# More block products and a written-out order in a fused attention and GLU kernel

## The chip, the cores and the metric

The kernel runs on one core of one Trainium2 chip. The metric is the device time of one execution in microseconds (us); a kernel's figure is the median of its runs. A core has TensorE (PE in the profile; it loads weights and multiplies), VectorE (DVE), ScalarE (ACT), GpSimd (POOL) and SyncE (SP), which here issues all DMAs. Each takes its own instructions strictly in order and waits for the others by semaphores.

## The reference, cut to what matters

```python
# x: 1 x 2048 x 512, H = 32 heads of 16, F = 1792, all bf16
xn = layernorm(x)
q, k, v = split(xn @ wqkv)                       # 512 -> 3 * 512
phi(t) = concat(softmax(t @ w_phi), softmax(-(t @ w_phi)))   # per head, 16 -> 32 features
kv = phi(k)^T v ; z = sum over tokens of phi(k)
attention = (phi(q) kv) / (phi(q) z + 1e-6)
glu = ((xn @ w_gate) * (xn @ w_up)) @ w_down     # 512 -> 1792 -> 512
out = x + attention @ wo + glu
```

`kv` sums over all 2048 tokens, so no attention output exists before the last token's k features do. The two GLU products are independent of the attention.

## The kernel before

The 2048 tokens are 16 tiles of 128 (`NT`), in four groups of 512 (`GT` = 4 tiles). The 512 channels are 4 chunks of 128 (`DC`), the 1792 hidden columns 14 chunks (`FC`), in two halves of 7 (`FH`). A matmul here has 128 x 128 weights and up to 512 columns; its f32 result goes to a PSUM bank, and six banks in turn (`bank`) serve most products.

The program is emitted in Python order, and each engine keeps the order in which its instructions were emitted (`manual_schedule`). In stages:

- **Start** (to about 12 us): layernorm of tiles 0 to 3, transposes, first v tiles, while weights arrive.
- **k stage** (lines 604 to 679): for each token tile `vkproj` projects v and k; `features` (lines 288 to 306) makes two exponentials on ScalarE (294, 296), a sum of 16 and a reciprocal on VectorE (300, 302) and the product on GpSimd (304); `kv(n)` adds to the two `kv` banks. Between them `ffn(1)` makes one unit of gate and up for groups 0 and 1 (28 units, `half`, line 350): four matmuls each of 512 columns for gate and for up, a copy on ScalarE (356) and a multiplication on VectorE (362). `weight_norm` (420, ScalarE) sums weights for power-of-two scales.
- **Attention and output**: `attend(n)` makes one tile's attention and sends it through a transposing DMA; `fin_parts(n)` (387) adds 14 matmuls of `w_down` and 4 of `wo`, all 512 columns wide, and stores a tile.
- **Block stage** (`run_blocks`): gate and up of groups 2 and 3 (tokens 1024 to 2047) use a two-by-two block product with seven products in place of eight (`pair_block`, line 487: two tokens' halves by two channel halves by two hidden halves). Its operands are differences: of weights, `T` (`weight_sums`, line 445, 28 steps of 512 columns on VectorE and GpSimd, after ScalarE has scaled the weights, 435), and of tokens, `ss` (454). The results are joined by copies on ScalarE (493, 495), additions on VectorE (499, 503) and, for the second factor, a multiplication from two SBUF operands on GpSimd or VectorE (504).
- **End**: output tiles 9 to 15, one `q_begin`/`attend`/`fin` round each; the last tile's output is stored in two pieces, of 384 and 128 columns.

Of the kernel before, what the change touches and what calls it, by code (L numbers as in the profile page):

```python
# [15 lines left out]
PSUM = bass.MemoryType.PSUM  # L16


def _bcast_ap(ap_in: bass.AP, new_ap):
    return bass.AP(tensor=ap_in.tensor, offset=ap_in.offset, ap=new_ap)  # L20


@with_exitstack
def kernel(
# [40 lines left out]
    consts = ctx.enter_context(tc.tile_pool(name="consts", bufs=1))  # L65
    wpool = ctx.enter_context(tc.tile_pool(name="wpool", bufs=1))
# [7 lines left out]
    wgu = wpool.tile([P, 2, DC, F], BF16)  # L74
# [60 lines left out]
    xnT = xpool.tile([P, DC, HALF], BF16)  # L135
# [11 lines left out]
    for i in range(NV):  # L147
        vt = vpool.tile([P, 8, 4, E1], BF16, name=f"vt{i}", tag="vt")
        nc.vector.memset(vt[:, :, :, DH:E1], 1.0)
        vts.append(vt)  # L150
# [9 lines left out]
    def bank(name, dt=F32, n=TT):  # L160
        return ps_s.tile([P, n], dt, name=name, tag="s")
# [3 lines left out]
    def xt(n):  # L165
        return xnT[:, :, n * P:(n + 1) * P] if n < QT else x16[:, :, (n - QT) * P:(n - QT + 1) * P]
# [21 lines left out]
    def subtract(n, *means):  # L188
        xns[n] = xnpool.tile([P, D], BF16, name="xn", tag="x")
        nc.vector.tensor_scalar(out=xns[n][:], in0=xall[:, n, :], scalar1=means[0],  # L190
                                scalar2=means[1] if len(means) > 1 else None, op0=ALU.subtract,
                                **(dict(op1=ALU.subtract) if len(means) > 1 else {}))
# [9 lines left out]
    def centre_by_halves(n):  # L202
        h = D // 2
        part = consts.tile([P, 2], F32)
        junk = xnpool.tile([P, 2, h], BF16, name="junk", tag="x")
# [5 lines left out]

    chores = []

    def chore(k=1):
        for _ in range(min(k, len(chores))):
            chores.pop(0)()

    def ln_block(lo):
        mv = mv_tile()
        nb = lnpool.tile([P, GT], F32, name="nb", bufs=GT)  # L220
        rstd = []

        def scales():
            r = lnpool.tile([P, GT], F32, name="rstd", bufs=GT)
            ln_rstd(mv, GT, r[:])
            nm = lnpool.tile([P, GT], F32, name="nm")
            nc.gpsimd.tensor_scalar(out=nm[:], in0=mv[:, :, 0], scalar1=-1.0, scalar2=None, op0=ALU.mult)
            nc.gpsimd.tensor_tensor(out=nb[:], in0=nm[:], in1=r[:], op=ALU.mult)
            rstd.append(r)

        def apply(i):
            late = lo + i >= QT
            xn = xnpool.tile([P, D], F16 if late else BF16, name="xn", tag="x")
            if late:
                nc.gpsimd.tensor_scalar(out=xn[:], in0=xall[:, lo + i, :], scalar1=rstd[0][:, i:i + 1],
                                        scalar2=nb[:, i:i + 1], op0=ALU.mult, op1=ALU.add)
            else:
                nc.scalar.activation(out=xn[:], in_=xall[:, lo + i, :], func=AF.Identity,
                                     scale=rstd[0][:, i:i + 1], bias=nb[:, i:i + 1])
            nc.sync.dma_start(out=xt(lo + i), in_=xn[:], transpose=True)  # L240

        for i in range(GT):
            chores.append(lambda i=i: ln_stats(lo + i, mv[:, i, :]))
        chores.append(scales)
        for i in range(GT):
            chores.append(lambda i=i: apply(i))
# [18 lines left out]
    def fold(qk, dst, j0):  # L265
        R = P // 2
        banks = [bank("pq").rearrange("p (j c x) -> p j c x", j=2, c=DC) for r in range(2)]
        for j in range(2):
            for c in range(DC):
                for r in range(2):  # L270
                    rows = slice(r * R, (r + 1) * R)
                    nc.tensor.matmul(banks[r][:, j, c, :], lhsT=wT2[rows, qk, c, (j0 + j) * P:(j0 + j + 1) * P],  # L272
                                     rhs=bd[rows, c, 4 * r:4 * r + 4, :].rearrange("p a b -> p (a b)"),
                                     start=True, stop=True)
        dv = dst[:, j0:j0 + 2, :].rearrange("p j (c r x) -> p r j c x", c=DC, r=2)
        nc.scalar.copy(out=dv[:, 0], in_=banks[0])
        nc.vector.tensor_copy(out=dv[:, 1], in_=banks[1])

    def fold_both(qk, dst):
        for j0 in (0, 2):  # L280
            fold(qk, dst, j0)
# [6 lines left out]
    def features(n, w, name, pf=None):  # L288
        if pf is None:
            pf = bank(name)  # L290
            proj(pf, n, w)
        e = epool.tile([P, NG, 2, 4 * DH], F32, name="e")
        pfv = pf.rearrange("p (g c) -> p g c", g=NG)
        nc.scalar.activation(out=e[:, :, 0, :], in_=pfv, func=AF.Exp,  # L294
                             scale=rst[:, n:n + 1] if n < GT else 1.0)
        nc.scalar.activation(out=e[:, :, 1, :], in_=pfv, func=AF.Exp,  # L296
                             scale=nrst[:, n:n + 1] if n < GT else -1.0)
        ev = e[:].rearrange("p g s (h f) -> p (g s h) f", f=DH)
        sums = epool.tile([P, 2 * H], F32, name="sums")
        nc.vector.tensor_reduce(out=sums[:], in_=ev, axis=AX.X, op=ALU.add)  # L300
        rs = epool.tile([P, 2 * H, 1], F32, name="rs")
        nc.vector.reciprocal(out=rs[:].rearrange("p a b -> p (a b)"), in_=sums[:])  # L302
        phi = epool.tile([P, NG, P], BF16, name=f"phi{name}", tag="phi", bufs=4)
        nc.gpsimd.tensor_tensor(out=phi[:].rearrange("p g (x f) -> p (g x) f", f=DH), in0=ev,  # L304
                                in1=rs[:].to_broadcast((P, 2 * H, DH)), op=ALU.mult)
        return phi

    sends = []

    def qproj(n, held=False, new_bank=bank):  # L310
        q_begin(n, new_bank)
        q_end(held)

    q_open = []

    def q_begin(n, new_bank):
        pf = new_bank("q")
        proj(pf, n, W1q, lower)
        q_open.append((n, pf))

    def q_end(held=False):
        q_rest()
        q_features(held)

    def q_rest():
        n, pf = q_open[0]
        proj(pf, n, W1q, upper)

    def q_features(held=False):
        n, pf = q_open.pop()  # L330
        phiq = features(n, W1q, "q", pf)

        def send():
            phiqTs[n] = qtpool.tile([P, NG, P], BF16, name="phiqT")
            nc.sync.dma_start(out=phiqTs[n][:], in_=phiq[:].rearrange("p g c -> p (g c)"), transpose=True)

        sends.append(send)
        if not held:
            qsend()

    def qsend():
        sends.pop(0)()

    hTs = {}
    units = [(T, f) for T in range(NGRP // 2) for f in range(FC)]

    def half(w, name, T, f, lo, hi):
        ps = bank(name)[:, 0:hi - lo]
        for c in range(DC):
            nc.tensor.matmul(ps, lhsT=w[:, c, f * P:(f + 1) * P], rhs=xnT[:, c, T * TT + lo:T * TT + hi],  # L350
                             start=(c == 0), stop=(c == DC - 1))
        return ps

    def gate_copy(ps, n):
        g_sb = gpool.tile([P, TT], BF16, name="g_sb")
        nc.scalar.copy(out=g_sb[:, 0:n], in_=ps)  # L356
        return g_sb

    def hidden(T, f, ps, g_sb, lo, hi):
        if T not in hTs:  # L360
            hTs[T] = hpool.tile([P, FC, TT], BF16, name="hT", tag="h")
        nc.vector.tensor_tensor(out=hTs[T][:, f, lo:hi], in0=ps, in1=g_sb[:, 0:hi - lo], op=ALU.mult)  # L362

    def unit(T, f, lo=0, hi=TT):
        pg = half(wg, "g", T, f, lo, hi)
        pu = half(wu, "u", T, f, lo, hi)
        hidden(T, f, pu, gate_copy(pg, hi - lo), lo, hi)

    def ffn(k):
        for _ in range(k):  # L370
            if units:
                unit(*units.pop(0))

    def fin_parts(n, new_bank, lo=0, hi=D):
        T, t4 = n // GT, n % GT
        w = hi - lo
        held = []

        rows = [(hTs[T][:, f, t4 * P:(t4 + 1) * P], wd[:, f, lo:lo + w]) for f in range(FC)]
        rows += [(oTs[n][:, c, :], wo[:, c, lo:lo + w]) for c in range(DC)]  # L380
        if n == 2 * GT:
            rows = [row for f, row in enumerate(rows) if f % FH != FH - 1 or f >= FC] + [rows[FH - 1], rows[FC - 1]]

        def mm(i):
            if i == 0:
                held.append(new_bank("fin")[:, 0:w])
            nc.tensor.matmul(held[0], lhsT=rows[i][0], rhs=rows[i][1], start=(i == 0), stop=(i == len(rows) - 1))  # L387
            if i == len(rows) - 1:
                store(held[0])
# [444 lines left out]
```

## Time and profile before

| | us |
|---|---|
| median of 3 runs | 216.08 |
| lowest and highest | 215.33, 216.12 |
| the profiled execution | 215.67 |
| its span, first to last instruction | 213.9 |
| PE busy in it | 210.1 (98%) |
| DVE, ACT, POOL busy | 163.2, 125.0, 129.2 |
| granted clock of TensorE | 1.00 |

The profile is one execution, by hardware trace. Its page gives busy time by engine and a chain of work that ended last; answers of the trace give groups of instructions (count, busy time, mean ns of one, idle time before them and what ended it), windows (busy time of each engine between two moments) and timelines (start, duration, engine, line, tiles). Consecutive instructions of an engine overlap a little, so their spacing, start to start, is shorter than the duration shown.

### The profile page before, as it was taken

The numbers are of one execution on the slowest core, as the hardware profiler recorded it, in microseconds if no ns is written. First come the engines' busy times: TensorE is split into PE (matmuls) and PEld (weight loads), VectorE is DVE, ScalarE is ACT, GpSimd is POOL, SyncE is SP. The second block draws the span as 40 slices with busy tenths as digits, with TensorE's granted clock in tenths as the row PEclk, the third lists the DMA queues.
The fourth block names the chain that finished last, engine by engine and source line by source line (L and its number), as shares of the span: only waits on it lengthen the run. The fifth ranks groups of instructions, "written<-read, shape, count | busy, mean of one in ns | idle before, by whom it ended". The sixth has DMA issues, their size and how long they took to land.

```text
span 213.9 us, 3610 instructions
## 1 busy us (share of the span) xinstructions
PE 210.1 (98%) x1280; PEld 101.7 (48%) x1280; DVE 163.2 (76%) x279; ACT 125.0 (58%) x219; POOL 129.2 (60%) x112
## 2 busy tenths in 40 slices
PE   8999999999999999999999999999999999999994
PEld 3664445444444444554444444444444444444543
DVE  5757979869867788887777897988969689776341
ACT  4635578998896999442666686868746352220000
POOL 3600557597895788859899497979788620333000
PEclk9999999999999999999999999999999999999999
DMA  5999995613022023234444202021120201333511
GB/s 152 266 281 385 374 287 87 91 26 75 0 51 52 0 49 81 66 40 112 100 101 100 49 0 52 0 74 25 48 49 3 74 26 34 91 98 98 126 49 49
DMA packets 47249, 19.91 MB, mean 93 GB/s; under 512 B 37504, under 2 KB 46976, under 8 KB 47104
## 3 DMA queue, kind: packets, MB, share of 16 engines
q1 hardware_dynamic: 47232, 19.69, 36.6%
q8 instruction: 10, 0.16, 0.3%
q14 instruction: 7, 0.06, 0.1%
HBM read 8.67 MB, written 2.10 MB: 50 GB/s over the span
## 4 chain that ended last, share of the span: by engine, by line
PE 98%; ACT 1%; DVE 0%; issue 0%
PE fin L387 29%; PE g L350 11%; PE u L350 11%; PE sa L487 11%; PE pv L285 7%; PE q L285 6%; PE k L285 6%; PE sc L487 6%; PE sb L487 3%; PE kv L622 2%; PE ab L686 2%; PE warm L554 2%; PE pq L272 1%; PE tp L253 1%; ACT k L493 0%; ACT xnT L256 0%
## 5 line engine op out<-in xcount | busy, mean ns | idle before, releaser
L387 PE MATMUL fin<-wd,hT 128*128 128x512 bf16 (+2 forms) x238 | 54.1, 366 | 0.0
L304 POOL TENSOR_TENSOR phiq<-e,rs 128x1024 bf16<-128x1024 f32 x16 | 30.9, 1934 | 25.6 <-DVE rs L302 18.1
L304 POOL TENSOR_TENSOR phik<-e,rs 128x1024 bf16<-128x1024 f32 x16 | 30.9, 1933 | 24.2 <-DVE rs L302 17.3
L300 DVE TENSOR_REDUCE sums<-e 128x64 f32<-128x1024 f32 x32 | 38.7, 1208 | 9.0 <-ACT e L296 9.0
L350 PEld LDWEIGHTS <-wgu 128*128 128x128 bf16 x240 | 23.1, 98 | 24.2
L387 PEld LDWEIGHTS <-hT 128*128 128x128 bf16 x238 | 22.3, 98 | 24.4
L350 PE MATMUL u<-xnT,wgu 128*128 128x512 bf16 (+1 forms) x120 | 29.1, 365 | 0.0
L350 PE MATMUL g<-xnT,wgu 128*128 128x512 bf16 (+1 forms) x120 | 28.9, 365 | 0.0
L504 POOL TENSOR_TENSOR hT<-u_sb,hT 128x512 bf16<-128x512 bf16 x18 | 21.1, 1185 | 10.1 <-DVE u_sb L503 10.1
L362 DVE TENSOR_TENSOR hT<-u,g_sb 128x512 bf16<-128x512 f32 (+1 forms) x30 | 18.6, 622 | 4.5 <-PE u L350 3.9
L356 ACT CAST g_sb<-g 128x512 bf16<-128x512 f32 (+1 forms) x30 | 17.1, 569 | 8.1 <-PE g L350 7.9
L294 ACT ACTIVATE e<-q 128x512 f32<-128x512 f32 x12 | 7.2, 598 | 23.6 <-PE q L285 23.6
L302 DVE RECIPROCAL rs<-sums 128x64 f32<-128x64 f32 x32 | 17.7, 552 | 2.5
L493 ACT ACTIVATE k<-sa,both 128x512 f32<-128x512 f32 x21 | 14.5, 688 | 8.7 <-PE sa L487 8.6
L495 ACT COPY k<-sa 128x512 f32<-128x512 f32 x21 | 12.3, 587 | 11.2 <-DVE u_sb L503 7.4
L398 DVE TENSOR_TENSOR o_sb<-fin,xall 128x512 bf16<-128x512 f32 (+2 forms) x13 | 8.4, 646 | 12.0 <-PE fin L387 12.0
L445 POOL TENSOR_TENSOR T<-wgu,T 128x512 f16<-128x512 bf16 x14 | 17.0, 1216 | 0.5
L387 PE MATMUL fin<-wo,oT 128*128 128x512 bf16 (+2 forms) x68 | 17.1, 366 | 0.0
L487 PEld LDWEIGHTS <-T 128*128 128x128 f16 x112 | 10.8, 98 | 13.1 <-issue 0.6
L487 PE MATMUL sa<-ss,T 128*128 128x512 f16 x56 | 16.7, 379 | 0.1
L435 ACT ACTIVATE wgu<-wgu,up 128x1024 bf16<-128x1024 bf16 x14 | 15.9, 1156 | 0.1
L420 ACT ACTIVATE junk<-wgu 128x1024 bf16<-128x1024 bf16 x14 | 15.1, 1083 | 0.0
(98 smaller groups left out, 352.1 us busy)
## 6 DMA issues: line engine op xcount, KB each, us to landing
out_dram<-o_sb SPq DMA_DIRECT2D x15, 128.0 KB, 1.9
wd<-in_B_w_down_dram SPq DMA_DIRECT2D x1, 1792.0 KB, 15.4
wgu<-in_B_w_gate_dram SPq DMA_DIRECT2D x2, 640.0 KB, 6.8
wgu<-in_B_w_up_dram SPq DMA_DIRECT2D x2, 640.0 KB, 8.0
xall<-in_A_x_dram SPq DMA_DIRECT2D x1, 1024.0 KB, 12.1
xall<-in_A_x_dram SPq DMA_DIRECT2D x4, 128.0 KB, 2.7
vk<-in_A_wqkv_dram SPq DMA_DIRECT2D x2, 256.0 KB, 3.6
wgu<-in_B_w_gate_dram SPq DMA_DIRECT2D x2, 256.0 KB, 4.9
```

Of the source, the lines that this page charges most:

```text
L285: nc.tensor.matmul(ps, lhsT=xt(n)[:, j, :], rhs=w[:, j, :], start=(j == 0), stop=(j == DC - 1))
L300: nc.vector.tensor_reduce(out=sums[:], in_=ev, axis=AX.X, op=ALU.add)
L302: nc.vector.reciprocal(out=rs[:].rearrange("p a b -> p (a b)"), in_=sums[:])
L304: nc.gpsimd.tensor_tensor(out=phi[:].rearrange("p g (x f) -> p (g x) f", f=DH), in0=ev, in1=rs[:].to_broadcast((P, 2 * H, DH)), op=ALU.mult)
L350: nc.tensor.matmul(ps, lhsT=w[:, c, f * P:(f + 1) * P], rhs=xnT[:, c, T * TT + lo:T * TT + hi], start=(c == 0), stop=(c == DC - 1))
L356: nc.scalar.copy(out=g_sb[:, 0:n], in_=ps)
L362: nc.vector.tensor_tensor(out=hTs[T][:, f, lo:hi], in0=ps, in1=g_sb[:, 0:hi - lo], op=ALU.mult)
L387: nc.tensor.matmul(held[0], lhsT=rows[i][0], rhs=rows[i][1], start=(i == 0), stop=(i == len(rows) - 1))
L435: nc.scalar.activation(out=cols, in_=cols, func=AF.Identity, scale=up2[:, k, g:g + 1])
L445: (nc.gpsimd if i % 2 or k < 2 else nc.vector).tensor_tensor(out=t[:, i], in0=a, in1=b, op=ALU.subtract)
L487: nc.tensor.matmul(held[name], lhsT=w[:, j, :], rhs=x[:, j, :], start=start and j == 0, stop=(j == hc - 1), skip_group_check=True)
L504: (nc.vector if k == FH - 1 else nc.gpsimd).tensor_tensor(out=dst, in0=u[:], in1=dst, op=ALU.mult)
```

## The change

The program is cut into 1,244 named steps, and a string `ORDER` gives the order in which they are emitted, with the engine of many of them (`/a` ScalarE, `/v` VectorE, `/g` GpSimd); `SLOTS` gives each step's buffer. The start, up to tile 3's v projection, is as before.

Three parts of the arithmetic change. Gate and up of group 1 (tokens 512 to 1023) no longer go through units; they use the seven block products too, on halves of 256 tokens (steps with `N`). Output tiles 9, 10, 11 are paired with 13, 14, 15 (`pair_steps`), and their `w_down` part becomes seven products over half the hidden chunks and half the output columns (256), from differences of `w_down` (`c`, `w` steps, f16) and of the hidden values (`S` steps, written over the gate and up weights). Their joins are `K`, `A`, `B` and `J` steps. The scales come from sums of squares and hold for a whole weight matrix, for `w_down` too. Third, the loop that emits the steps makes the first GpSimd instruction after a VectorE step with two SBUF operands wait for that step.

```diff
+ORDER = """
+wq g3 gc3/a =k g1 fk0 gc1/a fka0/v fk2 fkv0/a fkv2/a u3 u0 fka2/v k0 u1 k1 h1 h3 kx0 ky0 kr0 ki0 kp0/g g0 g4 ky1
...
+X15 P3a.10 J3.10 X10
+"""
...
+    def hidden_sum(i, k, eng):
+        tok = slice(t0 * P, TT)
+        S = [wgu16[:, j // 2, t0:GT, ((j % 2) * FH + k) * P:((j % 2) * FH + k + 1) * P] for j in range(4)]
+        A11, A12, A21, A22 = (hT(T)[:, k + h * FH, tok].rearrange("p (t x) -> p t x", x=P) for T in (2, 3) for h in (0, 1))
+        a, b, op = ((A21, A22, ALU.add), (S[0], A11, ALU.subtract), (A11, A21, ALU.subtract), (A12, S[1], ALU.subtract))[i]
+        eng.tensor_tensor(out=S[i], in0=a, in1=b, op=op)
...
+        product(1, "a", a(2, 0), d("b11"), True)
+        keep("k1", 1, "a")
+        add("k1", "A1", lambda: x(n, 0))
+        product(2, "b", a(2, FH), B21, True, (n, 0))
+        join(2, n, 0, "b", lambda: kept("k1"))
+        product(5, "d", s(0), d("t1"), True)
...
+        product(6, "a", s(1), d("t2"))
...
+        product(3, "c", s(3), d("b22"), True, (n, 1))
...
+        product(7, "a", s(2), d("t3"))
...
+        product(4, "a", a(3, FH), d("t4"), False, (m, 0))
...
+    both_in_sbuf = re.compile(r"(N?z|t|wt|c[bt]|S|N?m|[AB]|a|ws)\d")
+    turn = None
+    for word in ORDER.split():
+        name, _, eng = word.partition("/")
+        fn, default = steps.pop(name)
+        before = len(nc.cur_bb.bb.instructions)
...
+        issued = nc.cur_bb.bb.instructions[before:]
+        on_pool = [i for i in issued if i.engine == ET.Pool]
+        on_dve = [i for i in issued if i.engine == ET.DVE]
+        if on_pool and turn is not None:
+            tc.add_manual_dep(on_pool[0], turn.name, AFTER, reason="turns")
+            turn = None
+        if on_dve and both_in_sbuf.match(name):
+            turn = on_dve[-1]
...
-    blocks = [(k, g) for k in range(FH) for g in range(2)]
...
-        for n in range(9, NT):
-            if n < 12:
-                q_begin(n + 4, bank)
-                q_rest()
-            if n + 1 < NT:
-                attend(n + 1, ps_ab)
...
-            fin(n, cuts=(0, D) if n < NT - 1 else (0, 3 * P, D))
```

The steps that the prediction names: `vk` v and k projection of a tile, `vc` its copy, `kx ky kr ki kp kv` its features and `kv` sum (`q...` the same for q), `n` a weight norm, `a` a layernorm application, `gc` a gate copy, `p`/`k`/`j`/`m`/`d` products, copies, joins, multiplications of a block (`N` the narrow ones), `t` a weight difference, `P` a paired product (parts `a` and `b`, `w` for `wo`), `S`, `c`, `w` its operands, `f` parts of an ordinary output tile, `X` a store.

## The prediction

> **What bounds the kernel now.** I read the page first, then the chain that ended last, then windows of two stages, then the steps of one line.
>
> ```profile
> span 213.9 us, 3610 instructions
> PE 210.1 (98%) x1280; PEld 101.7 (48%) x1280; DVE 163.2 (76%) x279; ACT 125.0 (58%) x219; POOL 129.2 (60%) x112
> ...
> PE 98%; ACT 1%; DVE 0%; issue 0%
> ```
>
> The fourth line is the chain by engine: TensorE sets the end, from 9 us on almost without a hole. What shortens its column stream shortens the kernel, as long as nobody makes it wait. Its prices come from the chain in order of time (start, us, what):
>
> ```profile
> 12.33 0.44 PE u L350 x4
> 12.76 0.44 PE g L350 x4
> 13.20 0.44 PE u L350 x4
> ...
> 190.67 0.26 PE ab L686 x8
> 190.92 3.88 PE fin L387 x18
> ...
> 203.34 7.83 PE fin L387 x54
> ```
>
> 3.88/18 is 215.6 ns for 512 columns; 13.20 minus 12.33, over 8, is 108.7 ns for 256. The last row's 54 are 18 each of 512, 384 and 128 columns. So time follows columns, with some 2 ns for each matmul.
>
> Next, how much room the others leave. The windows cover the k stage's main part and the block stage (us; then PE, PEld, DVE, ACT and POOL busy, clock, DMA):
>
> ```profile
> 32.00:82.00 50.00, 50.00 (x350) 24.45 (x348) 40.58 (x63) 44.64 (x87) 38.53 (x32) 1.00 0.27 51
> 112.35:180.00 67.65, 67.56 (x341) 30.98 (x339) 56.99 (x90) 42.64 (x67) 48.08 (x38) 1.00 0.17 41
> ```
>
> ScalarE is at 89% in the first, VectorE at 84% in the second, and TensorE doesn't wait in either. Last, the weight differences (min/median/max ns):
>
> ```profile
> L445 POOL TENSOR_TENSOR T<-wgu,T x14: 1148/1155/1333, 107.9 to 163.7; 128x512 f16<-128x512 bf16 x14
> L445 DVE TENSOR_TENSOR T<-wgu x10: 414/894/1378, 122.8 to 161.2; 128x512 f16<-128x512 bf16 x10
> ```
>
> The same VectorE step takes 414 or 1378 ns. The timeline shows which: of each two, the first runs alone, and the second starts 0.2 us after a GpSimd multiplication of 1.26 us and ends 0.3 us after it. So a VectorE step on two SBUF operands that meets a GpSimd step in flight waits it out, up to 964 ns. VectorE's reductions (1.2 us, all alike) and its PSUM joins do not. The Trainium skill's page "SBUF — State Buffer", section "Who interferes with whom", says the same of two SBUF inputs: whoever issues first holds the shared ports for its whole instruction; the trace agrees, with 1378 against 414 ns.
>
> **TensorE's part.** Gate and up of tokens 512 to 1023: before, 14 x 8 = 112 matmuls of 512 columns, 24.15 us; after, 14 blocks x 7 products x 2 = 196 of 256, 21.31 us: -2.84. `w_down` of six tiles: 84 of 512, 18.11 us, become 3 pairs x 7 products x 7 = 147 of 256, 15.98 us: -2.13. The `wo` part is cut in two, 24 of 512 into 48 of 256: +0.04; one more norm sum, +0.05. Together **-4.9 us**. The list of the built program's instructions bears it out: 1452 matmuls for 1280, 12,537 columns fewer, which at 2.4 columns a ns (512 in 213) is 5.2 us, less 172 x 2 ns.
>
> A rule speaks against narrow products: "TensorE: Matmul & The Clock Gate", section "Back-to-back issue gap", in the Trainium skill, gives about 81 ns for a sustained 128-column matmul with its weight load, against 56 isolated; an estimate of 25 ns more for each of the 391 new ones would be 9.8 us. The trace disagrees at every width: 108.7 ns at 256 columns, 56 at 128, 32 at 68, each with its own 98 ns load.
>
> **The tail.** Before, TensorE ends at 211.17 and the span at 213.9: an o_sb step of 0.29 us on 128 columns and a 32 KB store. After, the last product P3a.10 is followed by a join of 256 columns (about 0.48: 743 ns at 512, less 0.26 for 256 columns) and a 128 KB store behind those of X11 and X15. +0.2 for the join and 0 to +0.4 for the store, whose 128 KB rows land after 1.9 us; I take **+0.3** in all. The start is as it was.
>
> So the floor, TensorE never waiting, is 215.67 - 4.9 + 0.3 = 211.1 against the profiled execution. That ran 0.4 below the median of the runs, so 211.5 as a median.
>
> **What the others must do for it.** Instructions grow from 279 to about 360 on VectorE, 219 to about 275 on ScalarE, 112 to about 155 on GpSimd. SP's 82 DMAs keep number and kind; only their order differs. I add up three stretches of the new order, by start-to-start spacing in the rows of before (two joins at 131.14 and 131.75: 0.61 us for a duration of 0.69), with 256 columns taken between the 512-column row and its fixed part.
>
> *k stage, vk4 to kv15.* TensorE: 39.1 us. ScalarE: 24 k exponentials x 0.485, 12 of q x 0.55, 10 weight norms x 1.15, 6 applications x 0.71, 11 v copies x 0.475, 3 gate copies x 0.465 = 40.6 us. GpSimd 37.3, VectorE 37.2. The units that filled TensorE here are half gone (their work now needs weight differences, later), so ScalarE is 104% of TensorE. Its excess of 1.5 us is paid unless it gets ahead earlier. ScalarE's idle share of before (11%) on top would make 45.6 us, 6.5 over; those gaps were waits for TensorE, so I take **+1.5**, bounds 0 and 6.5. Queued behind a late exponential are the sum, reciprocal and product of that tile and TensorE's kv step.
>
> *Block stage (=f to the last c copies).* TensorE 64.9. VectorE: 35 wide joins 22.1, 38 narrow 13.9, 14 direct products 6.4, q features 7.9, 24 steps with both operands in SBUF 7.3 if alone, others 2.3: 59.9, or 92%. Meetings with GpSimd (46.9 us, 72%) come on top: 24 x 0 to 0.96 us. Line 445's mean extra, 0.48, would make 11.5, so 71.4, 6.5 over. But each second step there met the GpSimd step that started after the first; the new wait holds that one back. It binds one way only: VectorE still waits out a GpSimd step already running. At 0.1 each VectorE has 62.3, within 64.9. The wait itself costs GpSimd: the rest of its queue (q products, differences for `p5` to `p7`) stands behind a VectorE step that may wait for TensorE. I take **+0.5**, bounds 0 and 6.5.
>
> *Paired stage to P7a.9.* TensorE 26.05. GpSimd: 12 `S` x 0.84, 5 `w` 6.35, 2 q products 3.8, 3 multiplications 2.8, 1 addition 0.6 = 23.6; VectorE's 17 two-operand steps take 5.4, and the two can't overlap: 29.0, or 3.0 over. But GpSimd idles for over a quarter of the stage before, and the last sums (S3) are wanted only near the end. I take 0, bounds 0 and 3.0. The added end chain, q product of tile 11, transposes (2.7 and 2.3 us to landing), attention, P2w.11, has about 3 us in hand by the same spacings.
>
> Sum: 211.5 + 1.5 + 0.5 = **213.5**.
>
> **The rivals.**
> - *Gap-free*: the order hides everything, 211.5. For it: before, ScalarE at 89% and VectorE at 84% cost TensorE nothing. Against: here 104% and 92%.
> - *The paired stage pays in full*: 213.5 + 3.0 = 216.5, no change. For it: `S` and `w` steps feed products that end the kernel, with little other TensorE work left. Against: GpSimd's earlier slack.
> - *VectorE becomes the bound of the block stage* (the slower side): each two-operand step costs 0.48 us. It decides from (64.9 - 59.9)/24 = 0.21 us a step; break-even with before, with ScalarE's 1.5 paid, is (5.0 + 216.1 - 213.0)/24 = 0.34. At 0.48: 211.5 + 1.5 + 6.5 = 219.5, or 218 without ScalarE's part. For it: GpSimd runs 72% of the time, and its steps last 0.6 to 1.9 us. Against: the wait that the change adds.
> - *Narrow matmuls show their weight load*: a quarter of 98 ns for 391 is 9.6 us, 223.1. The 108.7 ns row is against it.
>
> That the change doesn't do what it says is excluded by the instruction list.
>
> **How the numbers follow.** Forecast (212.5 to 215): 0.42; gap-free: 0.25; paired stage in full: 0.14; VectorE bound: 0.17; weight loads: 0.02. About 0.5% (1.1 us) can be told from no change, so under 215.0 is faster, 0.67; to 217.2 the same, 0.14; above it slower, 0.19. The range 210.8 to 219.5 runs from the floor, less the spread of the runs, to the VectorE case; weight loads, half of the VectorE case's tail and some below the floor are left out.
>
> **What would show it.** Right: PE busy near 204 to 207; 256-column products spaced 109 ns; TensorE's holes between 30 and 75 us, released by ScalarE; VectorE's two-operand steps mostly near 0.2 to 0.45 us. Wrong: those steps lengthened by 0.5 us or more and TensorE waiting for VectorE between 85 and 150 us; or holes after 170 us ended by GpSimd's `S` or `w` steps; or a tail beyond 3.3 us.

## The result, and the profile after

The changed kernel takes 226.83 us (median of 4 runs, 226.24 to 227.05) against 215.91 of the kernel before in the same comparison: a ratio of 1.051, 95% interval 1.048 to 1.054. The forecast was 213.5. The profiled execution took 226.24 us, 10.57 more than the one before.

The page of the changed kernel, its first lines, two rows of the 40 slices and the chain by engine:

```profile
span 224.5 us, 4155 instructions
PE 206.6 (92%) x1432; PEld 118.3 (53%) x1452; DVE 183.9 (82%) x361; ACT 154.1 (69%) x295; POOL 161.5 (72%) x158
...
PE   8999008999999999999999999999999999999993
PEclk9999956999999999999999999999999999999999
...
PE 71%; SPq 10%; POOL 7%; DMA 6%; issue 3%; DVE 2%; DVEq 0%
```

TensorE is busy for 3.5 us less than before, as meant, and yet the span is 10.6 us longer. Nearly all of the loss has one place: the two zeros, slices of 5.6 us each; the clock drops in the second of them and in the slice behind it. On the chain SyncE's queue and DMAs, absent before, now hold 16%. GpSimd's 7% is a stretch from 100.7 to 116.5 us, where TensorE itself waits only 0.4 us at its start and 0.3 us behind it.

TensorE's waits in the trace after (who, on whom: us in total, times, longest):

```profile
PE pq L471 <- DMA wT<-in_A_wqkv_dram: 11.4, 1, 11.4
PE warm L377 <- PEq L1092: 0.8, 1, 0.8
PE dc L960 <- DVE o_sb L989: 0.3, 1, 0.3
```

One wait makes up nearly all. `pq` is the fold of the q weights with `w_phi` (step `fq0`), small matmuls that need `wT`, the q weights as a transposing DMA delivers them. The timeline of TensorE there (start, us, what, the wait before it), then SyncE's queue of the same kernel, then that of the kernel before, and the first fold there:

```profile
21.86 1.03 PE L351 MATMUL u<-xnT,wgu 128*128 128x512 bf16 x4
34.26 0.61 PE L471 MATMUL pq<-bd,wT 64*128 64x64 bf16 x16 [11.37 <-DMA wT<-in_A_wqkv_dram]
...
39.19 0.41 PE L471 MATMUL pq<-bd,wT 64*128 64x64 bf16 x16
```

```profile
15.53 0.43 SPq L210 DMA_DIRECT2D wd<-in_B_w_down_dram  x1
16.01 8.33 SPq L211 DMA_DIRECT2D wo<-in_A_wo_dram  x1
24.39 7.82 SPq L491 DMA_TRANSPOSE wT<-in_A_wqkv_dram  x1
32.32 8.68 SPq L523 DMA_TRANSPOSE x<-xn  x3
```

```profile
16.44 8.24 SPq L110 DMA_DIRECT2D wo<-in_A_wo_dram  x1
28.67 6.58 SPq L240 DMA_TRANSPOSE xnT<-xn  x4
35.30 2.72 SPq L659 DMA_TRANSPOSE wT<-in_A_wqkv_dram  x1
```

```profile
55.74 0.41 PE L272 MATMUL pq<-bd,wT 64*128 64x64 bf16 x16
```

Before, the q weights were sent for at 35.3 us, landed at 40.9, and the fold ran at 55.7: 15 us in hand. The change moves the fold to 22.7 us (`u6 fq0 kv0` in `ORDER`) and the transfer to 24.4, the moment at which SyncE is through with issuing the load of `w_o`, behind `w_down`. `w_down` lands at 31.0 us, `w_o` at 32.5, and the q weights at 34.2. TensorE executes in order, so the gate and up products behind the fold, all ready, wait too.

The windows show the rest of the kernel (us; PE, PEld, DVE, ACT, POOL busy, clock, DMA share, GB/s):

```profile
20.00:40.00 20.00, 8.41 (x68) 3.92 (x68) 6.33 (x15) 8.11 (x16) 7.46 (x10) 0.74 0.81 228
40.00:60.00 20.00, 19.89 (x120) 9.58 (x121) 18.59 (x33) 18.35 (x36) 16.04 (x18) 1.00 0.22 45
60.00:80.00 20.00, 19.84 (x146) 10.21 (x148) 18.83 (x25) 19.65 (x38) 18.66 (x11) 1.00 0.27 54
...
120.00:140.00 20.00, 19.95 (x126) 12.08 (x126) 18.91 (x41) 17.19 (x38) 17.71 (x19) 1.00 0.00 1
```

From 40 us on TensorE is nearly as full as it was (19.5 us or more of each 20 up to 200 us), with ScalarE at 98% in the third row and VectorE at 95% in the last.

### The profile page after: what moved, and what is told of

It reads as the page before. It is cut to its first block, busy times and chain, and to the rows that moved or that the text cites. A ratio compares the mean times of both kernels' runs of the same rounds, so it can differ in the third digit from the quotient of the medians.

```text
span 224.5 us, 4155 instructions
## 1 busy us (share of the span) xinstructions
PE 206.6 (92%) x1432; PEld 118.3 (53%) x1452; DVE 183.9 (82%) x361; ACT 154.1 (69%) x295; POOL 161.5 (72%) x158
## 4 chain that ended last, share of the span: by engine, by line
PE 71%; SPq 10%; POOL 7%; DMA 6%; issue 3%; DVE 2%; DVEq 0%
PE fin L678 15%; PE sa L824 13%; PE sc L824 7%; PE q L337 6%; PE k L337 5%; PE pv L337 4%; DMA wT<-in_A_wqkv_dram 4%; PE u L351 4%; SPq L211 4%; PE da L960 3%; PE g L351 3%; PE sb L824 3%; SPq L187 2%; PE kv L590 2%; DMA oT<-otok 2%
## 5 line engine op out<-in xcount | busy, mean ns | idle before, releaser
L678 PE MATMUL fin<-wd,hT 128*128 128x512 bf16 (+2 forms) x150 | 37.1, 359 | 0.2
L846 POOL TENSOR_TENSOR hT<-u_sb,hT 128x512 f16<-128x512 bf16 (+1 forms) x29 | 26.8, 936 | 5.8 <-DVE hT L846 2.1
L357 ACT COPY k<-sa 128x512 f32<-128x512 f32 (+1 forms) x42 | 19.9, 480 | 7.3 <-PE sa L824 5.1
L359 ACT ACTIVATE k<-sa 128x512 f32<-128x512 f32 (+1 forms) x39 | 18.9, 499 | 7.4 <-PE sa L824 4.2
L678 PEld LDWEIGHTS <-hT 128*128 128x128 f16 (+1 forms) x154 | 14.2, 98 | 11.2
L337 PE MATMUL k<-vk,x 128*128 128x512 bf16 x47 | 17.8, 379 | 0.1
L337 PE MATMUL pv<-vk,x 128*128 128x512 bf16 x46 | 17.4, 379 | 0.1
L839 DVE SCALAR_TENSOR_TENSOR hT<-sc,k 128x512 f16<-128x512 f32 (+1 forms) x28 | 15.1, 546 | 1.8 <-PE sc L824 0.9
L843 DVE TENSOR_TENSOR u_sb<-sc,k 128x512 bf16<-128x512 f32 (+1 forms) x28 | 15.0, 550 | 0.8 <-PE sc L824 0.3
L351 PE MATMUL u<-xnT,wgu 128*128 128x512 bf16 (+1 forms) x63 | 15.0, 372 | 0.2 <-issue 0.2
```

The lines of the kernel that those rows point to most:

```text
L337: nc.tensor.matmul(ps, lhsT=xt(n)[:, j, :], rhs=w[:, j, :], start=(j == 0), stop=(j == DC - 1))
L357: A.copy(out=dst, in_=src)
L359: A.activation(out=dst, in_=src, func=AF.Identity, scale=scale)
L678: nc.tensor.matmul(held["fin", n, lo], lhsT=l, rhs=r, start=len(done) == 1, stop=len(done) == FC + DC)
L839: V.scalar_tensor_tensor(out=h(*to), in0=mine[ps], scalar=gate_scale, in1=mine[kept][:], op0=ALU.mult, op1=ALU.add)
L846: eng.tensor_tensor(out=h(*to), in0=mine["u", i][:], in1=h(*to), op=ALU.mult)
```

## The experiments

The expectations name two theories. **W**: the loss is TensorE standing in order behind a fold whose operand comes late, and SyncE's queue ahead of that operand; the rest is hidden. **V**: the 11 us hole also lets ScalarE, VectorE and GpSimd get ahead, so that their excess (the prediction's 1.5 and 0.5 us) is only covered by it and appears when it goes. Every ratio is to the kernel before, run on the same chip in between.

**The hole alone, in the kernel before.** The q weights' DMA right behind that of `w_o`, and the first q fold behind the k projection of tile 1:

```diff
     nc.sync.dma_start(out=wo[:], ...)
+    nc.sync.dma_start(out=wT2[:, 0, :, :], in_=A_wqkv[:, 0:D], transpose=True)
...
         kproj(1)
+        fold(0, W1q, 0)
...
-        nc.sync.dma_start(out=wT2[:, 0, :, :], in_=A_wqkv[:, 0:D], transpose=True)
...
-            if n in (9, 10):
-                fold(0, W1q, 2 * n - 18)
+            if n == 10:
+                fold(0, W1q, 2)
```

> Edit, on the kernel before: the q weight DMA is issued right behind wo's load, and the first q fold is emitted behind kproj(1), at about 24.7 us of TensorE, instead of in the k stage; nothing else. Theory W: the fold waits until about 34.3, a hole of 9.6 us, and the slow clock adds 1 to 2: about 226 to 227.5. If the hole belongs to the new order's other steps: 217 or less.

Measured: 227.76 us, ratio 1.054 (1.051 to 1.058). Its TensorE timeline has the same hole:

```profile
34.45 0.61 PE L273 MATMUL pq<-bd,wT 64*128 64x64 bf16 x16 [9.75 <-DMA wT<-in_A_wqkv_dram]
34.99 0.61 PE L351 MATMUL g<-xnT,wgu 128*128 128x512 bf16 x1
```

None of the change's arithmetic is in this kernel, and moving one fold and its transfer forward costs it as much as the whole change costs. Theory W holds for the size.

**The clock's part.** Fifty 512-column matmuls on constants into the fold's own bank, ahead of the fold in the changed kernel:

```diff
+            if name == "q" and j0 == 0:
+                for _ in range(50):
+                    nc.tensor.matmul(raw[0], lhsT=ones[:, 0:P], rhs=ones, start=True, stop=True)
```

> Edit: 50 matmuls of 512 columns on constants (10.8 us) into fq0's own bank ahead of the fold, so that TensorE is busy during its wait; their result is overwritten. Theory W with a clock part: the fold still waits to 34.2, but the granted clock stays at 1.00 and the matmuls after it run 216 ns instead of 426: about 1.9 us less, 224.9. If the clock costs nothing: 226.8. If the wait itself were caused by something that TensorE's work feeds, the time would grow by up to 10.8 us.

Measured: 224.60 us (224.49 to 224.72), 2.2 below the changed kernel. The fold, what follows it and the second fold:

```profile
34.10 0.41 PE L471 MATMUL pq<-bd,wT 64*128 64x64 bf16 x16 [0.24 <-DMA wT<-in_A_wqkv_dram]
...
34.70 2.75 PE L347 MATMUL u<-xnT,wgu 128*128 128x512 bf16 x11
37.39 0.41 PE L471 MATMUL pq<-bd,wT 64*128 64x64 bf16 x16
```

The fold starts within 0.2 us of where it did, so little but the rate afterwards has changed: 512 columns take 216 ns here from 34.7 us on, and 426 from 35.2 to 37.8 us in the changed kernel. From the first fold to the second it is 3.3 us here and 4.9 there.

**The fold late, the transfer as it is.**

```diff
-... u6 fq0 kv0 ... fqv0/a ... fqa0/a ... fq2 ... fqv2/a ... fqa2/a ...
+... kv4 fq0 fqv0/a fqa0/a vk10.0 ... kv7 fq2 fqv2/a fqa2/a ...
```

> Edit: only the two q weight folds (fq0, fq2 and their copies) are emitted later, behind kv4 and kv7; the q weight DMA stays where it was. Theory W (the in-order TensorE stands 11.4 us at fq0 for a DMA queued behind all loads, and runs some 1.9 us slower after it; all else is nearly gap-free): the 11.4 and 1.9 go, but the x4 transposes stand behind the same DMA in SP's queue (first one landed at 34.8), and vk4.0 would now come at about 30.3, so 4.5 us come back as a new hole: 226.8 - 13.3 + 4.5 = about 218. Theory V (VectorE and ScalarE, 92 to 98% busy from 40 to 120 us, are the bound, and the hole only hid their debt): 221 or more, TensorE's holes between 40 and 150 us ended by ACT and DVE. Theory N (no debt and no new hole): 213.5.

Measured: 224.06 us (222.44 to 225.62), ratio 1.037 (1.030 to 1.045). TensorE's two long waits, in the trace of a run of 222.44 us:

```profile
PE pv L333 <- DMA x<-xn: 5.0, 1, 5.0
PE pq L467 <- ACT e L533: 2.0, 1, 2.0
```

The fold no longer waits for its weights, but TensorE now waits 5.0 us for tile 4's transposed tokens, which stand behind the q weights in SyncE's queue, and 2.0 us at the fold's new place for a bank that ScalarE has yet to read. The slow clock follows the first of them. About 3 of 11 us come back. W's 218 us had the first wait (4.5 us), and had neither the second nor the slow clock; the time is in V's range, but the long wait is not V's.

**The transfer early, the fold as it is.** It goes right behind the k weights' transposing transfer:

```diff
     nc.sync.dma_start(out=wT2[:, 1, :, :], in_=A_wqkv[:, D:2 * D], transpose=True)
+    nc.sync.dma_start(out=wT2[:, 0, :, :], in_=A_wqkv[:, 0:D], transpose=True)
```

> Edit: only the DMA of the q weights is issued earlier, right behind that of the k weights; the order of all compute steps is that of the changed kernel. It lands near 15 us instead of 34.2, and the loads behind it some 1.8 us later. Theory W: no wait at fq0; x4's first transpose lands near 33.3 to 34, vk4.0 is ready at about 31.3, a hole of about 2.5 us is left: 226.8 - 13.3 + 2.5 = about 216. Theory V: 220 or more, holes between 40 and 150 us ended by ACT and DVE.

Measured: 218.86 us, ratio 1.016 (1.010 to 1.023). TensorE's waits:

```profile
PE pv L334 <- DMA x<-xn: 2.3, 1, 2.3
PE g L348 <- DMA wgu<-in_B_w_gate_dram: 1.3, 1, 1.3
PE warm L374 <- PEq L1085: 0.8, 1, 0.8
PE pq L468 <- DMA wT<-in_A_wqkv_dram: 0.5, 1, 0.5
```

Issued at 11 us, the weights land at 15.6, and the q fold, at 24.8 us, waits for nothing. The 0.5 us in the last row are the k fold's, at 13.5 us, whose weights land 0.8 us later than in the changed kernel. What the q weights push back now comes late in its turn: a gate load, and the tokens of tile 4, behind `w_down` and `w_o`. One line moved takes away 7 to 8 of the 11 us. W's 216 had the wait for tile 4; it lacked the one for the gate load, and the slow clock (512 columns in 426 ns from 37.0 to 40.0 us).

**Fold and transfer late, `w_down` and `w_o` still first.** The folds as in the kernel with the late fold, and:

```diff
-wq g3 gc3/a ...
+g3 gc3/a ... xt5 wq a10/a ...
```

> The changed kernel with the q folds and the q weights' transfer emitted later (the transfer behind those of tiles 4 to 7), but the transfers of w_down and wo still ahead of all of these, as in both kernels. Theory W: TensorE is free of the fold, and what is left is the wait of tile 4's v projection for its transposing transfer, behind w_down and wo in SyncE's queue (landing at about 34 to 36 us in the kernel with the later folds, 5.2 us of hole): transfers issue 8 us earlier than there, so 0 to 3 us of hole and 211.5 to 215. If the wait is for the bandwidth of w_down and wo rather than for the q weights ahead in the queue: 5 us of hole as there, 217 to 219.

Measured: 219.45 us (218.19 to 220.48), ratio 1.015 (1.012 to 1.019). Tile 4's tokens, with no q weights ahead of them, are still 2.2 us late: they were sent for at 27.4 us and land from 33.2 on, after `w_o` at 32.8. So `w_down` and `w_o` alone hold back a transfer that this order wants earlier than the old one did. The hole is of the size that W expected; the time is above W's range, since the late fold also waits 2.3 us for its bank.

**Tokens of tiles 4 to 7 first, then q weights, `w_down`, `w_o`.**

```diff
-    nc.sync.dma_start(out=wd[:], ...)
-    nc.sync.dma_start(out=wo[:], ...)
...
-wq g3 gc3/a ...
+g3 gc3/a ... xt5 wq wd wo a10/a ... kv2 fq0 fqv0/a fqa0/a ... xt12 fq2 fqv2/a fqa2/a ...
```

> The changed kernel with SyncE's loads in the order in which they are wanted: the transposing transfers of tiles 4 to 7 first, then the q weights, then w_down and wo; and with the two q folds emitted later (behind the kv step of tile 2, and behind the transfers of tile 12). Theory W (the loss is TensorE standing in order behind the q weights, and SyncE's queue in front of them; all later stages are hidden): no hole over 2 us before 40 us, the granted clock at full speed from 12 us, 211.1 + 0.4 to 1.5 for new small holes, so 211 to 213, faster than both kernels. Theory V (TensorE's hole let ScalarE and VectorE work ahead, and their excess of 1.5 and 0.5 us or more shows once it is gone): TensorE waits for ScalarE between 40 and 75 us or for VectorE between 85 and 150 us, 214 to 218.

Measured: 227.80 us, ratio 1.055 (1.051 to 1.058): a clear miss. Tile 4 is in time, and the two loads now stand in front of tiles 8 to 11. A row of ScalarE and the queue:

```profile
46.96 1.06 ACT L712 ACTIVATE junk<-wgu 128x1024 bf16<-128x1024 bf16 x1 [9.14 <-DMA x<-xn]
```

```profile
36.39 0.57 SPq L485 DMA_DIRECT2D wd<-in_B_w_down_dram  x1
37.01 1.02 SPq L489 DMA_DIRECT2D wo<-in_A_wo_dram  x1
38.13 8.30 SPq L525 DMA_TRANSPOSE x<-xn  x4
```

The weight norm on ScalarE writes its squares into a buffer of the same ring as `xn`, so it must wait until the transposing transfer has read that buffer. The transfer, issued behind `w_down`, lands at 46.9 us, right after `w_down` (44.9) and `w_o` (46.3). ScalarE's q cast stands behind the norm, and TensorE's next v projection waits 8.8 us for the bank of that cast. I had looked at who needs the transfers' results, and not at who waits for the buffers they read.

**`w_down` and `w_o` behind the tokens of tiles 8 to 11.** The q weights stay where the change has them:

```diff
-... xt8 g11 ...
+... xt8 wd wo g11 ... kv2 fq0 fqv0/a fqa0/a ... vk10.1 fq2 fqv2/a fqa2/a ...
```

> The changed kernel with the q weights' transfer where it was, but w_down and wo loaded behind the transposing transfers of tiles 8 to 11 (first wanted at about 52 us by a weight norm, and those transfers at about 40 us no longer stand behind them), and the two q folds emitted later (behind the kv step of tile 2 and behind the k projection of tile 10). Theory W (only transfers wanted by TensorE and ScalarE that stand behind w_down and wo, or the q weights, cost time; ScalarE's and VectorE's excess is hidden): no hole over 1 us after 12 us, 211 to 213, faster than before and changed. Theory V (ScalarE's 1.5 us and VectorE's 0.5 us show once the start has no hole): TensorE waits for ScalarE between 40 and 75 us and for VectorE between 85 and 150 us, 213.5 to 216. Should the transposing transfers be slow for another reason than the loads ahead of them: a hole at 30 us or 40 us as in the kernels before it, 217 and more.

Measured: 215.31 us (12 runs), ratio 0.998 (0.997 to 1.000). The big hole and the slow clock are gone; in their place ScalarE makes TensorE wait:

```profile
37.24 0.39 PE L465 MATMUL pq<-bd,wT 64*128 64x64 bf16 x15 [0.28 <-ACT vt L351]
40.22 0.38 PE L331 MATMUL pv<-vk,x 128*128 128x512 bf16 x1 [0.76 <-ACT W1q L351]
48.95 0.41 PE L465 MATMUL pq<-bd,wT 64*128 64x64 bf16 x16 [0.29 <-ACT e L539]
```

These are holes of the kind that V foretold, and the time is in V's range; W had 211 to 213.

**Is it ScalarE's load, or where I put the folds?** Two kernels on top of that one: the four casts of the folds on VectorE, and the folds in banks that have long been free.

```diff
-fqv0/a fqa0/a ... fqv2/a fqa2/a
+fqv0/v fqa0/v ... fqv2/v fqa2/v
```

> The kernel with w_down loaded late, with the four casts of the two q folds on VectorE in place of ScalarE (2.2 us less on ScalarE between 36 and 52 us). If the holes left there (0.28 and 0.76 us at 37 to 40 us, released by ScalarE's v copy and q cast, 0.29 at 48.9 by its exponentials) are ScalarE's load, as the prediction's term of 1.5 us has it: about 1 us less of hole, 214.0 to 214.6. If VectorE, which is the fuller in 20 to 40 us, then makes the wait: the same holes released by VectorE, 215 to 216.

```diff
-kv2 fq0 (banks 1, 2) fqv0/a fqa0/a ... vk10.1 fq2 (banks 1, 4) fqv2/a fqa2/a
+kv2 fq0 (banks 0, 1) fqv0/v fqa0/v ... vk9.1 fq2 (banks 4, 1) fqv2/a fqa2/v
```

> The same, with the folds in PSUM banks that have been free for longer (banks 0 and 1 at the first, with both casts on VectorE; behind the projection of tile 9 at the second, banks 4 and 1, one cast on each engine). If the holes come from where these folds were put, and not from an engine's load: no hole over 0.3 us between 36 and 55 us, 213 to 214, faster than before by over 0.5%. If they are load, they move to the next wait: 214.5 to 216.

Measured: 214.87 us, ratio 0.996 (0.994 to 0.997), and 214.98 us, 0.996 (0.995 to 0.997). Both are 0.4% faster than the kernel before, where the kernel above was 0.2% faster. Page and waits of the first:

```profile
span 212.8 us, 4175 instructions
PE 206.8 (97%) x1452; PEld 117.9 (55%) x1452; DVE 186.1 (87%) x365; ACT 152.4 (72%) x291; POOL 161.5 (76%) x158
```

```profile
PE pq L465 <- ACT e L539: 0.5, 1, 0.5
PE kv L592 <- POOL phik L561: 0.3, 1, 0.3
PE ab L629 <- DMA phiqT<-phiq: 0.3, 1, 0.3
PE pv L331 <- DVE hT L365: 0.2, 1, 0.2
PE sa L826 <- DVE T L776: 0.2, 1, 0.2
```

The holes do not go; they move to ScalarE, GpSimd and VectorE in turn (in the second kernel to two waits for VectorE's casts, 0.9 us, and ScalarE's exponentials, 0.3). So it is not one engine or one bank. That it is the load of all three in this stage fits this, and is not shown: no run takes work away from all three.

**The turns.** The wait of GpSimd's next instruction taken out, in the changed kernel and in the kernel with the tokens of tiles 4 to 7 first:

```diff
-        if on_dve and both_in_sbuf.match(name):
+        if False and on_dve and both_in_sbuf.match(name):
```

> The changed kernel without the turns alone. Theory W: the hole of 11.5 us at 22.7 us and the slow clock behind it stay, so 226 to 228; any difference from the changed kernel is what the turns are worth there. If the turns themselves were the loss (GpSimd's queue held back): 217 or less.

> The kernel with the loads in order, without the turns (GpSimd no longer waits for a VectorE step on two SBUF operands). If the turns are worth what the row of the weight differences gives (0.48 us for each of 24 steps, with 5 us of slack to lose first): 6.5 us slower than with them, TensorE waiting for VectorE between 85 and 150 us. If a wait on either engine is hidden because VectorE and GpSimd run ahead of TensorE: within 1 us of the kernel with the turns, with VectorE's two-operand steps at 0.8 us and more and TensorE without a wait for them.

Measured: 238.02 us, ratio 1.103 (1.100 to 1.106), and 238.26 us (five runs), 1.101 (1.097 to 1.104). Without the turns both kernels are some 11 us slower, so the turns are not what the changed kernel loses by. VectorE's steps on two SBUF operands (min/median/max ns), first with turns, then without:

```profile
L846 DVE TENSOR_TENSOR hT<-u_sb,hT x13: 273/283/801, 119.7 to 197.2; 128x256 f16<-128x256 bf16 x7, 128x512 f16<-128x512 bf16 x6
L774 DVE TENSOR_TENSOR T<-wgu,T x6: 415/418/803, 126.3 to 167.6; 128x512 f16<-128x512 bf16 x6
```

```profile
L842 DVE TENSOR_TENSOR hT<-u_sb,hT x13: 347/752/2015, 123.4 to 212.4; 128x256 f16<-128x256 bf16 x7, 128x512 f16<-128x512 bf16 x6
L770 DVE TENSOR_TENSOR T<-wgu,T x6: 409/1080/1377, 131.5 to 178.3; 128x512 f16<-128x512 bf16 x6
```

In the trace without them TensorE waits for VectorE:

```profile
PE sa L820 <- DVE T L770: 2.4, 1, 2.4
PE sc L820 <- DVE hT L852: 2.2, 1, 2.2
PE ab L623 <- DVE otok L650: 1.9, 2, 1.1
PE fin L674 <- DVE u_sb L839: 1.6, 1, 1.6
```

## Why the prediction was wrong, step by step

**The step that failed** is two sentences: "The start is as it was", and "SP's 82 DMAs keep number and kind; only their order differs". The first read `ORDER` only down to tile 3's v projection; the second took an order for harmless. Neither asked, for the two folds that `ORDER` moves from 55.7 and 59.9 us to 22.7 and later, when their operand lands. The trace of before held what was needed: `w_o` occupies SyncE's queue until 24.7 us, a transposing transfer behind it takes some 5 us to land (28.67 to 33.3), so the q weights could not be there before about 30 us, 7 us after the fold's turn, and every matmul behind it would wait. None of the four rivals had a place in the start, and the loss fell outside the range; that the weight-load rival's 223.1 us lies nearest to the measured time is chance.

**The books.** From the span's start to TensorE's end it is 211.16 us before and 221.13 after, +9.97. Columns: -4.9. The fold's wait: +11.4. The slow clock: +2.2, by the medians of this kernel and of the one with the hole filled (1.6 of it between the two folds). Three waits for VectorE at 100, 118 and 215 us, by the spacings of the matmuls there: 0.38 + 0.32 + 0.42 = +1.1. Sum: +9.8, and 0.2 is not accounted for. The tail, 3.4 us for 2.8, brings the span's 10.6.

**TensorE's part: right.** In the kernel with the casts on VectorE the trace holds every one of the 1452 matmuls. Its spacings beyond the price of each width (215.6, 108.7, 55.7 ns and so on) add up to 6.72 us, those of before to 3.58. TensorE ends at 209.41 for 211.16, and -1.75 less 3.14 is -4.9, the prediction's figure. PE busy was forecast at 204 to 207 and is 206.6 in the changed kernel, whose trace lacks 20 matmuls, and 206.8 here; the weight-load rival is dead.

**The tail: right in kind, too small.** +0.6 us, with +0.3 taken; it passes the 3.3 us that the prediction named as a limit, by 0.1.

**k stage, ScalarE's 1.5 us: right in size, in part by luck, and hidden here.** In the changed kernel ScalarE works at 98% and TensorE doesn't wait. The hole explains this: in it the other engines ran out of work, VectorE for 12.9 us, ScalarE for 11.5, GpSimd for 10.5. With the hole gone, the spacings between 30 and 60 us are 1.4 us longer in the kernel with the casts on VectorE than before. The prediction put it on ScalarE alone; the waits are for three engines. And its sum for this stage didn't hold the four casts of the folds, some 2 us of work, which the later folds of that kernel bring into it.

**Block stage, 0.5 us, and the VectorE rival.** The forecast took 0.1 us extra for each two-operand step, and had the rival decide from 0.21. Undisturbed, the 13 multiplications take 0.34 us on the mean (0.28 each for seven of 256 columns, 0.42 for six of 512). With the turns they average 0.37, and TensorE hardly waits. Without them they average 0.80, 0.45 us more than undisturbed, where the rival had 0.48 from the row of the weight differences: its price of a step was right. Its total of 6.5 us was low; the turns are worth 11. The paired stage's steps lengthen too (the 512-column differences of `w_down` take some 1.0 us for 0.4), and waits of 2.2 us and more slow TensorE's clock (0.91 between 120 and 160 us). So what the new wait does was read rightly. In the kernel with the casts on VectorE, this stage and the ones after it cost 1.6 us more than before (waits for `phiqT`, `T` and `o_sb`), with 0.5 taken.

**Paired stage, 0: right.** TensorE is busy for over 19.8 of each 20 us from 160 to 200 us in the changed kernel; an `S` step on GpSimd took 0.91 us for 0.84. The end chain behind it, with 3 us in hand by the prediction, had less: the wait of 0.42 us at 215 us is there. VectorE stood 0.8 us at an attention step for a transposing transfer that took 4.5 us to land, and its output step came late for it.

Put together, without the missed step the sum of 213.5 would have been short by 1.1 here and 0.3 in the tail: 214.9, half a per cent below the kernel before, and not 1.2. The kernel with the casts on VectorE takes 214.87 us, but the corrections were read from its own trace, so this is bookkeeping and no independent test.

## What to carry to other kernels

When a step is moved forward, ask of each operand when it lands, and which queue it stands in and behind what; on engines that execute in order one late operand of a small step stops everything behind it. Moving a load is the same question again from the other end: what is now behind it, and who waits for the buffers which those transfers read. And a large hole hides other debts, so its removal returns less than its length.

## What the runs showed of the hardware

- A transposing DMA issued behind large plain loads landed only after them: the q weights at 34.2 us behind `w_o` at 32.5, tile 4's tokens at 33.2 behind 32.8 with the q weights sent later, tile 9's at 46.9 behind 46.3 with the loads in order. The q weights took 9.8 us from the start of their issue behind `w_down` and `w_o` (24.4 to 34.2), and 4.6 us at 11 us, ahead of them. The issue of `w_o` itself held SyncE for 8.3 us with many loads outstanding, and for 0.9 to 1.0 us when it was sent at 37 or 40 us. Whether the queue's depth or the bandwidth does this was not told apart.
- After a hole TensorE runs at half rate: spacing 426 ns for 512 columns in place of 215.6, until 37.8 us in the changed kernel, 3.5 us after the hole's end. The Trainium skill's page "TensorE: Matmul & The Clock Gate", section "What's actually happening", has the gate go to half rate after an idle window of about 3.4 us; the hole of 11.4 us agrees. But waits shorter than that window, of 2.2 to 2.4 us, were followed by it too in five of six cases here, up to 1.1 us after the wait; those of 2.0 us and less in none: by these runs a wait of 2.2 us can already cost the clock.
- VectorE's multiplications on two SBUF operands took 0.45 us more on the mean (0.80 for 0.34) where GpSimd steps could run beside them, and letting GpSimd wait for such steps was worth 11 us of 238.
